# Transposing token rows a second time in float32r, and adding the scaled difference to them

## The chip, the cores and the metric

The kernel runs on one core of one Trainium2 chip. The core has a matrix engine (TensorE, PE in the profile, its weight loads listed apart as PEld), a vector engine (VectorE, DVE), a scalar engine (ScalarE, ACT), a general one (GpSimd, POOL) and a queue that issues transfers (SyncE, SP). Each engine works through its own instructions in order, and semaphores make one wait for another. The metric is the device time of one execution in microseconds.

## What is computed

Eight batches of eight heads of causal attention with a decay from the gates f, over 576 tokens with 64 dimensions a head; then, on the 4608 tokens with their 512 features, a layer norm, two weight matrices with a ReLU between them, and a residual.

```python
scores = np.matmul(q, k.transpose(0, 1, 3, 2)) / np.sqrt(D)
cum = np.cumsum(np.log(np.clip(f, 0.0001, 1.0)), axis=-1)
scores = np.where(causal, -1e9, scores + cum[..., :, None] - cum[..., None, :])
attn = np.exp(scores - scores.max(-1, keepdims=True))
attn = attn / (attn.sum(-1, keepdims=True) + 1e-09)
x = matmul(attn, v)                       # then [tokens, heads * D]
xn = (x - mu) / np.sqrt(var + 1e-06) * g_ln
out = x + np.maximum(xn @ w_ch1, 0.0) @ w_ch2
```

All inputs are float32 but for the two weight matrices, which come as 64-bit floats.

## The kernel before

**Precision.** Most products are made of three float32r products (high times high, high times low, low times high), with each operand split into a rounded high part and the rest. float32r is a second type of four bytes; the kernel rounds an operand into it to get the high part. The first twelve heads use plain float32 or a mixture.

**The attention stage** is a loop over units: 64 heads with four units each, in order. A unit makes the scores of a block of query rows (`qk_mm`, L371 and L372), the mask and the row minimum on VectorE (`softmax_a`, L395), the exponential on ScalarE (L406), the row factor on VectorE (L411, L412), the scaling of the probabilities on GpSimd (L413), their transposes on TensorE two units later (`transpose_unit`, through `tr`, L419), the copies of those on ScalarE (L469) and their low parts on VectorE (L474), and the product with v one unit after that (`av_unit`, L504). Finished heads go to DRAM with features on rows, tokens along the columns (`xd1`, `xd2`).

**The expert stage** (class `Moe`) works through 18 chunks of 256 tokens and is woven into the units: each unit from the 35th on also carries one of a chunk's 16 steps. A step is twelve products into a tile h (`mm1`, L581 to L583), a ReLU on ScalarE (L589), the low part on VectorE (L594), and six products into two accumulators (`mm2`, L603 to L605). A chunk's operand x is loaded from DRAM and split (`chunk_split`, L565 on ScalarE and L566 on VectorE), the last two of its four parts right ahead of the chunk's first step. After the last unit a short loop makes the steps that are left, alone.

**The rows.** The residual and the variance need the tokens with tokens on partitions. After the 9th and the 11th step of a chunk `rows_load` fetches 128 tokens into `xw`, after the 11th and the 13th `chunk_rows` transposes them: four 128x128 transposes into one PSUM bank xp (through `tr`, L419), a copy to xt on ScalarE (L628), and the statistics on VectorE (L633, L634). In all 36 times. After the 13th step `chunk_rstd` queues the fourteen small VectorE operations of the reciprocal root, of which each unit runs up to six; `chunk_out` (L662) scales the accumulators, adds xt and sends the rows out.

**The order** of the work inside a unit is written by hand, as a string of letters. From the 70th unit on it is the last of these; R is the place of `chunk_rows` and of the splits of x, B of the row factor, t of the transposes, A of the product with v, M and N of a step's two groups of products:

```python
    (70, "WwAthQFlMSPNgreamLRB"),
```

**PSUM.** Two banks hold the accumulators. The six others are handed out in turn by `bank`, to scores (s), transposes (tr, xp), products with v (o) and steps (h); a tile waits until the readers of the bank's last tile are done.

```python
    def bank(name):
        return ps.tile([P, 512], F32, tag="b", bufs=6, name=name)
```

`identr` is the identity in float32r, and `ident` the same bytes read as float32. The weights are decoded and split during the first 270 us or so, on ScalarE, VectorE and GpSimd.

Of the kernel before, what the change touches and what calls it, by code (L numbers as in the profile page):

```python
# [8 lines left out]
F32 = mybir.dt.float32  # L9
F32R = mybir.dt.float32r  # L10
# [3 lines left out]
ALU = mybir.AluOpType  # L14

B, H, S, D = 8, 8, 576, 64
DM, DFF = H * D, 4 * H * D
P = 128
KT = DM // P
# [40 lines left out]
def attn_moe(ctx: ExitStack, tc: tile.TileContext, qk, v, f, g, w1, w2, out):  # L60
    nc = tc.nc
# [7 lines left out]
    late = ctx.enter_context(tc.tile_pool(name="late", bufs=1))  # L69
# [3 lines left out]
    def bank(name):  # L73
        return ps.tile([P, 512], F32, tag="b", bufs=6, name=name)

    def m2(name, dt):
        return work.tile([P, 512], dt, tag="m2", bufs=11, name=name)


    identr = const.tile([P, P], F32R, tag="identr", name="identr")  # L80
# [6 lines left out]
    for i in range(WARM):  # L87
# [4 lines left out]
        out=mask[:, S - P :], in_=mask[:, S - P :], pattern=[[-1, P]], base=0,  # L92
# [42 lines left out]
    class WPrep:  # L135
# [132 lines left out]
        late = None  # L268
# [148 lines left out]
    def tr(out_, in_):  # L417
        m = in_.shape[0]
        nc.tensor.transpose(out_, in_, ident[:m, :m])  # L419
# [202 lines left out]
    def chunk_rows(c, i):  # L622

        tp = bank(f"xp{c.n}_{i}")
        for k in range(KT):
            tr(tp[:, P * k : P * k + P], c.xw[:, k, :])
        xt = m2(f"xt{c.n}_{i}", F32)
        nc.scalar.copy(out=xt, in_=tp)  # L628
        if i == 0:
            c.sv = work.tile([P, 2, 2], F32, tag="sv", bufs=2, name=f"sv{c.n}")  # L630
            c.rs = work.tile([P, 4], F32, tag="rs", bufs=2, name=f"rs{c.n}")
        bs = work.tile([P, 6], F32, tag="bs", bufs=2, name=f"bs{c.n}_{i}")
        nc.vector.bn_stats(bs, xt)  # L633
        nc.vector.bn_aggr(c.sv[:, i, :], bs)  # L634
        c.xt.append(xt)
# [30 lines left out]
    class Moe:  # L666
# [62 lines left out]
        def rest(self):  # L729
            c, self.step = self.step, None  # L730
            if c is not None:
                self.prev = (c, c.pend)
                if c.j in (FT - 5, FT - 3):
                    chunk_rows(c, (c.j - (FT - 5)) // 2)
                if c.j in (FT - 7, FT - 5):
                    rows_load(c, (c.j - (FT - 7)) // 2)
                if c.j == FT - 3:
                    chunk_rstd(c)
            self.fetch()
# [160 lines left out]
```

## Time and profile before

| | us |
|---|---|
| median of two runs | 1233.5 (1232.73 to 1234.27) |
| the profiled execution | 1235.2 |
| its span, first to last instruction | 1233.4 |
| TensorE busy | 1209.6 |
| VectorE busy | 763.8 |
| ScalarE busy | 647.0 |
| GpSimd busy | 425.6 |

A profile shows one execution. A group's row gives the source line, engine, operation, output and inputs by the names in the program, the shape, how many there were, then the busy time in microseconds, the mean of one in nanoseconds, the idle time of the engine just before them, and what ended that. A row of the timeline gives start, duration and instruction, merged where several of one kind follow each other ("x4"), with idle time ahead of it in square brackets. TensorE's instructions overlap in the pipeline: the distance from one start to the next says what an instruction costs in a row of them, its own duration does not. L12 is line 12 of the kernel.

The share of busy time in 40 slices of the span shows the stages: weights and attention in the first nine or so, attention with steps up to the 33rd, steps alone behind that.

```profile
PE   7998999899999999999999999999999999999998
DVE  5777647576767667676767676858676765233232
ACT  5887655455556555555555555656555653112111
POOL 3558544234343334344434333434434330000000
PEclk8998999999999999999999999999999999999999
```

### The profile page before, as it was taken

What the parts mean: (1) busy time and instruction counts of PE and PEld (TensorE: products, weight loads), DVE (VectorE), ACT (ScalarE), POOL (GpSimd) and SP (SyncE); (2) the same over time, 40 slices, a digit from 0 to 9 for tenths busy, and PEclk for the clock granted to TensorE, in tenths of its full rate; (3) what the DMA queues carried; (4) which work ended last, traced back from release to release, by engine and by line L of the source; (5) the groups of instructions that cost most, each with busy time, mean ns of one, the idle gap of its engine ahead of it and who ended that gap; (6) DMA issues with size and microseconds to landing.
All of it is one profiled execution on the core that took longest, in us unless ns stands there. A gap on an engine that the chain in (4) does not pass through costs nothing.

```text
span 1233.4 us, 25519 instructions
## 1 busy us (share of the span) xinstructions
PE 1209.6 (98%) x8140; PEld 1079.6 (88%) x8140; DVE 763.8 (62%) x2884; ACT 647.0 (52%) x1920; POOL 425.6 (35%) x533
## 2 busy tenths in 40 slices
PE   7998999899999999999999999999999999999998
PEld 5665889789999999999999999999999999999997
DVE  5777647576767667676767676858676765233232
ACT  5887655455556555555555555656555653112111
POOL 3558544234343334344434333434434330000000
PEclk8998999999999999999999999999999999999999
DMA  6877644444544454455444545545444553443533
GB/s 174 248 231 226 209 146 136 128 162 141 156 144 155 155 172 155 149 164 168 143 143 150 166 155 160 164 126 175 141 145 148 162 155 97 138 132 112 151 110 95
DMA packets 138358, 190.78 MB, mean 155 GB/s; under 512 B 31216, under 2 KB 80624, under 8 KB 138224
## 3 DMA queue, kind: packets, MB, share of 16 engines
q1 hardware_dynamic: 138224, 189.15, 49.7%
q8 instruction: 65, 1.06, 0.4%
q14 instruction: 69, 0.57, 0.2%
HBM read 157.46 MB, written 23.36 MB: 147 GB/s over the span
## 4 chain that ended last, share of the span: by engine, by line
PE 91%; DVE 3%; DMA 2%; ACT 2%; SPq 1%; issue 1%; POOL 0%; DVEq 0%; ACTq 0%; POOLq 0%
PE h L581 11%; PE h L582 11%; PE h L583 11%; PE acc L603 11%; PE acc L604 10%; PE acc L605 10%; PE tr L419 7%; PE o L504 6%; PE s L371 3%; PE s L372 3%; PE o L482 3%; PE s L369 2%; DMA raw<-in_qk_dram 1%; PE xp L419 1%; PE pc L190 1%; DMA wr<-in_w_dram 1%
## 5 line engine op out<-in xcount | busy, mean ns | idle before, releaser
L413 POOL TENSOR_SCALAR p<-p,st 64x64 f32<-64x64 f32 (+4 forms) x320 | 172.2, 541 | 550.2 <-DVE st L412 203.5
L581 PE MATMUL h<-x,w1h 128*128 128x256 f32 x1152 | 330.3, 287 | 5.6 <-DVE st L411 4.1
L582 PE MATMUL h<-x,w1h 128*128 128x256 f32 x1152 | 326.2, 283 | 0.7 <-DVE st L411 0.6
L583 PE MATMUL h<-x,w1l 128*128 128x256 f32 x1152 | 325.4, 282 | 0.0
L589 ACT ACTIVATE hh<-h 128x256 fp32r<-128x256 f32 x288 | 110.5, 384 | 280.2 <-PE h L583 276.2
L594 DVE SCALAR_TENSOR_TENSOR hh<-h,hh 128x256 fp32r<-128x256 f32 x288 | 121.6, 422 | 188.9 <-ACT hh L589 183.5
L603 PE MATMUL acc<-w2h,hh 128*128 128x512 f32 x576 | 228.1, 396 | 0.0
L581 PEld LDWEIGHTS h<-x,w1h 128*128 128x128 f32 x1152 | 218.6, 190 | 10.6 <-DVE st L411 4.3
L604 PE MATMUL acc<-w2s,hh 128*128 128x512 f32 x576 | 226.8, 394 | 0.0
L605 PE MATMUL acc<-w2h,hh 128*128 128x512 f32 x576 | 226.2, 393 | 0.0
L582 PEld LDWEIGHTS h<-x,w1h 128*128 128x128 f32 x1152 | 218.8, 190 | 4.2 <-DVE x L566 1.1
L583 PEld LDWEIGHTS h<-x,w1l 128*128 128x128 f32 x1152 | 218.5, 190 | 0.0
L406 ACT ACTIVATE p<-p,st 64x64 f32<-64x64 f32 (+4 forms) x320 | 178.3, 558 | 56.7 <-DVE st L395 53.7
L469 ACT CAST ph<-tr 64x128 fp32r<-64x128 f32 (+4 forms) x416 | 117.9, 332 | 127.3 <-PE tr L419 98.3
L419 PE MATMUL tr<-identr,p 128*128 128x128 f32 (+1 forms) x896 | 141.8, 275 | 2.6 <-POOL p L413 2.5
L395 DVE CUSTOM_DVE_ANT_0 p<-s,mask 64x64 f32<-64x64 f32 (+4 forms) x320 | 130.4, 420 | 8.8 <-PE tr L419 2.8
L474 DVE TENSOR_TENSOR ph<-tr,ph 64x192 fp32r<-64x192 f32 x208 | 62.6, 301 | 113.1 <-ACT ph L469 110.2
L605 PEld LDWEIGHTS acc<-w2h,hh 128*128 128x128 f32 x576 | 108.4, 188 | 25.6 <-DVE st L411 0.2
L419 PEld LDWEIGHTS tr<-identr,p 128*128 128x128 f32 (+1 forms) x896 | 101.7, 131 | 26.0 <-POOL p L413 5.9
L604 PEld LDWEIGHTS acc<-w2s,hh 128*128 128x128 f32 x576 | 109.3, 190 | 12.4
L603 PEld LDWEIGHTS acc<-w2h,hh 128*128 128x128 f32 x576 | 109.0, 189 | 12.5
L371 PE MATMUL s<-hi 128*64 128x64 f32 x336 | 110.2, 350 | 5.2 <-POOL hi L349 5.2
(82 smaller groups left out, 1790.9 us busy)
## 6 DMA issues: line engine op xcount, KB each, us to landing
w2s<-w2d SPq DMA_DIRECT2D x288, 256.0 KB
raw<-in_qk_dram SPq DMA_DIRECT2D x56, 576.0 KB
wr<-in_w_dram SPq DMA_DIRECT2D x32, 512.0 KB
vr<-in_v_dram SPq DMA_DIRECT2D x64, 160.0 KB
out_dram<-xt SPq DMA_DIRECT2D x36, 256.0 KB
xq<-hi SPq DMA_DIRECT2D x56, 144.0 KB
xa<-xs SPq DMA_DIRECT2D x32, 160.0 KB
w2d<-wl SPq DMA_DIRECT2D x16, 256.0 KB
```

What stands on the lines that cost most here:

```text
L371: mm(sp, h.hi[:, 0, q0 : q0 + m], h.hi[:, 1, a:z], start=True, stop=False)
L395: nc.vector.tensor_tensor_reduce(out=pt[:m, a:z], in0=sp, in1=mask[:m, off + a : off + z], scale=-SCALE, scalar=3.0e38 if i == 0 else st[: ...
L406: nc.scalar.activation(pt[:m, :w], pt[:m, :w], AF.Exp, bias=st[:m, i : i + 1], scale=-1.0, accum_out=st[:m, 2:3])
L413: nc.gpsimd.tensor_scalar(out=pt[:m, :w], in0=pt[:m, :w], scalar1=st[:m, 3:4], scalar2=1.0, op0=ALU.mult, op1=ALU.mult)
L419: nc.tensor.transpose(out_, in_, ident[:m, :m])
L581: mm(ph, w1h[:, k, fs], c.x[k][:, 0, :], start=(k == 0), stop=False)
L582: mm(ph, w1h[:, k, fs], c.x[k][:, 1, :], start=False, stop=False)
L583: mm(ph, w1l[:, k, fs], c.x[k][:, 0, :], start=False, stop=(k == KT - 1))
L594: nc.vector.scalar_tensor_tensor(out=h[:, 1, :], in0=ph, scalar=0.0, in1=h[:, 0, :].bitcast(F32), op0=ALU.max, op1=ALU.subtract)
L603: mm(c.acc[i], h[:, 0, ts_], w2h[:, j, :], start=(j == 0), stop=False)
L604: mm(c.acc[i], h[:, 0, ts_], low, start=False, stop=False)
L605: mm(c.acc[i], h[:, 1, ts_], w2h[:, j, :], start=False, stop=(j == FT - 1))
```

## The change

`chunk_rows` transposes the same rows a second time, into a second bank xq, with data, identity and output declared as float32r. VectorE then subtracts xt, the copy of the first transposes, from it, multiplies the difference by 2^20 and adds it to xt, ahead of the statistics. `dif` is a new SBUF tile of its own.

```diff
         tp = bank(f"xp{c.n}_{i}")
         for k in range(KT):
             tr(tp[:, P * k : P * k + P], c.xw[:, k, :])
+        tq = bank(f"xq{c.n}_{i}")
+        for k in range(KT):
+            nc.tensor.transpose(tq[:, P * k : P * k + P].bitcast(F32R), c.xw[:, k, :].bitcast(F32R), identr)
         xt = m2(f"xt{c.n}_{i}", F32)
         nc.scalar.copy(out=xt, in_=tp)
+        dif = late.tile([P, DM], F32, tag="dif", bufs=1, name=f"dif{c.n}_{i}")
+        nc.vector.tensor_tensor(out=dif, in0=tq, in1=xt, op=ALU.subtract)
+        nc.vector.scalar_tensor_tensor(out=xt, in0=dif, scalar=2.0**20, in1=xt, op0=ALU.mult, op1=ALU.add)
         if i == 0:
```

TensorE's order around the first half of chunk 5 (acc are the accumulators, o the product with v of head 31, tr the transposes of head 32). Before:

```order
L605 MATMUL acc5_1_6641<-w2h_126,hh5_9_7113 128x512
L419 MATMUL xp5_0_7172<-identr_74,xw5_0_7050 128x128 x4
L504 MATMUL o31_4_7198<-ph2_31_7066,vv31_6986 128x256 x4
L504 MATMUL o31_4_7198<-ph2_31_7066,vv31_6986 128x128
L504 MATMUL o31_4_7198<-pl2_31_7067,vv31_6986 64x256 x3
```

Changed:

```order
L605 MATMUL acc5_1_6721<-w2h_126,hh5_9_7193 128x512
L419 MATMUL xp5_0_7252<-identr_74,xw5_0_7130 128x128 x4
L629 MATMUL xq5_0_7257<-identr_74,xw5_0_7130 128x128 x4
L504 MATMUL o31_4_7286<-ph2_31_7146,vv31_7066 128x256 x4
L504 MATMUL o31_4_7286<-ph2_31_7146,vv31_7066 128x128
L504 MATMUL o31_4_7286<-pl2_31_7147,vv31_7066 64x256 x3
```

The four new transposes stand between the old ones and the product with v; nothing else moves.

VectorE's order at the same place (bs and sv are the statistics, st the row factors, ph and pl the transposed probabilities). Before:

```order
L594 SCALAR_TENSOR_TENSOR hh5_10_7168<-h5_10_7144,hh5_10_7168 128x256
L633 BN_STATS bs5_0_7181<-xt5_0_7177 128x6
L634 BN_AGGR sv5_7179<-bs5_0_7181 128x2
L411 TENSOR_SCALAR st32_2_7158<-st32_2_7158 128x1
L412 RECIPROCAL st32_2_7158<-st32_2_7158 128x1
```

Changed:

```order
L594 SCALAR_TENSOR_TENSOR hh5_10_7248<-h5_10_7224,hh5_10_7248 128x256
L633 TENSOR_TENSOR dif5_0_7264<-xq5_0_7257,xt5_0_7262 128x512
L634 SCALAR_TENSOR_TENSOR xt5_0_7262<-dif5_0_7264,xt5_0_7262 128x512
L639 BN_STATS bs5_0_7269<-xt5_0_7262 128x6
L640 BN_AGGR sv5_7267<-bs5_0_7269 128x2
L411 TENSOR_SCALAR st32_2_7238<-st32_2_7238 128x1
L412 RECIPROCAL st32_2_7238<-st32_2_7238 128x1
```

The two new operations stand ahead of the statistics, and so ahead of the row factors of the unit.

## The prediction

> **What bounds the kernel now.** I read the page's head and its chain of waits first, then the busy time by stretch, then who waited on TensorE, and only then single places.
>
> ```profile
> span 1233.4 us, 25519 instructions
> ...
> PE 1209.6 (98%) x8140; PEld 1079.6 (88%) x8140; DVE 763.8 (62%) x2884; ACT 647.0 (52%) x1920; POOL 425.6 (35%) x533
> ...
> PE 91%; DVE 3%; DMA 2%; ACT 2%; SPq 1%; issue 1%; POOL 0%; DVEq 0%; ACTq 0%; POOLq 0%
> ```
>
> The chain that ended last runs on TensorE (PE) for 91% of the span. The next view gives busy time by stretch: length, then PE, weight loads (PEld), VectorE (DVE), ScalarE (ACT), GpSimd (POOL), the granted clock, and DMA.
>
> ```profile
> 280.00:1030.00 750.00, 749.92 (x5297) 690.93 (x5296) 520.42 (x2015) 432.81 (x1310) 289.64 (x366) 1.00 0.49 153
> 1030.00:1233.00 203.00, 199.67 (x1291) 181.47 (x1289) 60.11 (x184) 36.67 (x94) 0.00 (x0) 1.00 0.41 121
> ```
>
> From 280 us on PE has no gap worth the name, in the attention stage (to 1030 us) or behind it. What PE ever waited for lies earlier, and the two longest entries of its waits are small:
>
> ```profile
> PE s L371 <- POOL hi L349: 5.2, 2, 3.6
> PE h L581 <- DVE st L411: 4.1, 1, 4.1
> ```
>
> So a microsecond added to PE's queue is a microsecond on the end, nearly everywhere. The changed step, the rows' transposes, stands in that queue 36 times: 18 chunks of two 128-token halves, four transposes each.
>
> **The change, part 1: four more transposes on PE, 36 times.** First the form that is there already, by line and shape, then the chain around 509 us.
>
> ```profile
> L419 PE MATMUL xp<-identr,xw 128*128 128x128 f32 x144 | 21.6, 272 | 0.0
> 508.83 0.44 PE xp L419 x4
> 509.27 0.95 PE o L504 x9
> ```
>
> One transpose is listed with 272 ns, but they overlap: in the chain four of them take 0.44 us, 0.11 each, and the next group starts right behind. The float32r form is not in the trace. Its pieces are: a float32r weight load of 128 columns, and 128 moving columns in float32r.
>
> ```profile
> 502.06 0.27 PE L372 MATMUL s<-kl,xq 66*128 66x192 f32 x1
> 502.17 0.31 PE L581 MATMUL h<-x,w1h 128*128 128x256 f32 x1
> 502.08 0.19 PEld L581 LDWEIGHTS h<-x,w1h 128*128 128x128 f32 x1
> 502.19 0.19 PEld L582 LDWEIGHTS h<-x,w1h 128*128 128x128 f32 x1
> L504 PE MATMUL o<-pl,vv 128*64 128x128 f32 x104 | 23.1, 222 | 0.0
> 509.64 0.57 PE L504 MATMUL o<-pl,vv 128*64 128x256 f32 x4
> 510.05 0.27 PE L419 MATMUL tr<-identr,p 128*64 128x128 f32 x1
> ```
>
> The first four are float32r products and loads. Loads of 128 columns follow each other at 0.11 us, and a product with only 192 moving columns is also followed after 0.11 (502.06 to 502.17), while 64 columns fewer should have bought something: the load paces it. The last three give the other end. Four float32r products with 64-column loads span 0.57 us; the last is one of 0.222, so it starts at 509.64 + 0.57 - 0.222 = 509.99, and the next instruction starts at 510.05, 0.06 us later. So a float32r transpose costs 0.11 us if its load takes the usual step or if it moves its data as the float32 one does, and 0.06 if neither holds. I take 0.11: both nearest rows, the transpose and the 128-column load, give it, and 0.06 needs a load of half the width.
>
> PE's term: 36 x 4 x 0.11 = 15.8 us; lower end 36 x 4 x 0.06 = 8.6 us. None of it is hidden after 280 us (32 of the 36 halves); of the four earlier ones one sits ahead of the 4.1 us wait above and may vanish, 0.4 us at most.
>
> The Trainium skill ("TensorE: Matmul & The Clock Gate", Part 4: PE-mode transpose) gives about 275 ns for one 128x128 transpose inside a kernel. The 272 ns above agree with it as a duration. Taken as PE's time for each, it would make 144 x 0.275 = 39.6 us, an estimate from that page; the chain's 0.44 us for four speaks against using it so.
>
> **Part 2: two VectorE operations, 36 times.** The subtraction reads one PSUM and one SBUF operand of 128x512; the multiply-add reads two from SBUF.
>
> ```profile
> L474 DVE TENSOR_TENSOR pl<-tr,ph 128x384 fp32r<-128x384 f32 x104 | 58.0, 558 | 2.4
> L474 DVE TENSOR_TENSOR pl<-tr,ph 128x256 fp32r<-128x256 f32 x52 | 22.1, 425 | 1.6
> L662 DVE SCALAR_TENSOR_TENSOR xt<-acc,rs,xt 128x512 f32<-128x512 f32 x36 | 25.5, 745 | 2.0 <-PE acc L605 2.0
> ```
>
> 128 columns more cost 558 - 425 = 133 ns, so the subtraction is 558 + 133 = 691 ns; the multiply-add I price as L662, 745 ns. Together 1.43 us, 51.7 us in all. DVE goes from 764 to 815 us, 65% of the longer span: on average there is room. The place matters more. Around the second half of one chunk (ACT copy, DVE, PE, by time):
>
> ```profile
> 518.01 0.59 ACT L628 COPY xt<-xp 128x512 f32<-128x512 f32 x1 [0.54 <-PE xp L419]
> 518.63 0.69 DVE L633 BATCH_NORM_STATS2 bs<-xt 128x6 f32<-128x512 f32 x1 [1.65 <-ACT xt L628]
> 519.61 0.16 DVE L412 RECIPROCAL st<-st 128x1 f32<-128x1 f32 x1
> 519.96 0.75 POOL L413 TENSOR_SCALAR p<-p,st 128x576 f32<-128x576 f32 x1 [5.08 <-DVE st L412]
> 519.06 0.30 PE L581 MATMUL h<-x,w1h 128*128 128x256 f32 x1
> 521.89 0.60 PE L419 MATMUL tr<-identr,p 128*64 128x128 f32 x4
> 522.00:532.00 10.00, 10.00 (x73) 9.31 (x72) 9.27 (x38) 6.72 (x23) 4.96 (x6) 1.00 0.25 71
> 531.33 0.75 DVE L566 TENSOR_TENSOR x<-xr,x 128x256 fp32r<-128x256 f32 x2
> 531.80 0.39 PE L582 MATMUL h<-x,w1h 128*128 128x256 f32 x1
> DVE ph L474 <- ACT ph L469: 0.8, 1, 0.8
> DVE hh L594 <- ACT hh L589: 0.5, 1, 0.5
> ```
>
> DVE waits 1.65 us for the ACT copy ahead of the statistics, so it arrives there on time whatever the first half cost it. Then it has 2.3 us of work where it had 0.9, and 1.43 us more stand ahead of two hand-overs to PE.
>
> The first is the tightest. The row statistics (L412) release GpSimd's normalisation of the probabilities, which ends at 519.96 + 0.75 = 520.71; PE transposes them at 521.89, 1.18 us later. There is no idle time on this way, so GpSimd ends 1.43 us later, and PE, itself 0.44 later by then, finds 1.18 - 1.43 + 0.44 = 0.19 us left. It holds, barely, at the second half of each chunk.
>
> The second: behind 522 us DVE is nearly full, 9.27 of 10 us. At the end of that stretch the next chunk's operand x is split (L566, two of them; the first ends about 531.33 + 0.375 = 531.7) and PE reads it at 531.80, 0.1 us later. The lateness of 1.43 - 0.44 = 0.99 us shrinks by DVE's idle time on the way; the last two rows are DVE's waits between 510 and 538 us apart from those for the copy, 0.8 + 0.5 = 1.3 us, so x should come in time.
>
> Both margins are a tenth or two wide. I allow 0.5 us in all for chunks where they fail. Upper end: half of 0.99 us in each of the 13 chunks of the attention stage, 6.4 us; lower end 0, since nothing here can make PE's work shorter. Behind 1030 us DVE is busy for 60 of 203 us and covers the 1.43 us.
>
> **Part 3: one more PSUM buffer per half.** The six shared banks go round faster: between xp and the next use of the same bank there is one tile fewer. The bank of xp is wanted next by the h tile at 519.06, and the copy that frees it ends at 518.60; PE comes 0.44 us later now, so that gap grows. The bank of xq is free when the subtraction ends, 518.63 + 0.69 = 519.32, and the next tile in it is written at 521.89 (plus 0.44). Cost 0. If the copy were later by a microsecond, PE would stall that long at 519.06.
>
> Part 4: nothing is added on ACT, POOL or the DMA queue, and nothing is moved past another instruction. ACT's copy waits for xp alone, not for xq.
>
> **The sum.** 15.8 + 0.5 + 0 = 16.3 us. The profiled execution took 1235.2 us (span 1233.4 and 1.8 around it), which gives 1251.5; it stands 1.7 us above the median of 1233.5, so against the median the forecast is 1249.8 us, 1.3% slower. A measurement of this kernel can tell about 2% (24.7 us) from no change, so this counts as within it.
>
> **Rivals.**
> - *The fast transpose.* Float32r needs one pass and a short load: 0.06 us each, 8.6 us, 1242.1. For it: the 64-column rows above. Against it: every 128-column float32r load here steps at 0.11.
> - *DVE takes over (slower).* If DVE's idle time on the way is not really idle, because ACT and DVE wait on each other in turn, each of the 26 halves of the attention stage (13 chunks) shows its 0.99 us on PE: 25.7 us more, 1275. For it: 9.27 of 10 us busy, and margins of 0.19 and 0.1 us. Against it: 1.3 us of waits on the way, and a DVE that is 70% busy over the stage (520 of 750 us). It decides from 0.34 us a half, when 1249.3 passes 1258.2.
> - *Transposes that do not overlap.* Each float32r transpose holds PE for its 272 ns: 144 x 0.272 = 39.2 us, 1272.7. This is what the Trainium skill's 275 ns (same page and part as above) would come to. Against it: float32 transposes overlap, and so do float32r products.
> - *It is hidden.* PE's ends are modelled, so its 749.92 of 750 us could contain slack: 1233.5. For it: the loads are busy for 691 of 750 us only. Against it: the chain steps from one matmul to the next without a gap.
>
> **How the numbers follow.** 0.11 us a transpose with stalls below 6.4 us: 0.68, and its own range is 1249 to 1256. Fast transpose: 0.16. DVE takes over: 0.09. No overlap: 0.04. Hidden: 0.03. The range 1241 to 1256 holds the first two (0.84) and leaves out the rest (0.16); its low end is the fast transpose's 1242 and 1 us for the run-to-run spread, its high end 1249.3 + 6.4. Slower by over 2%: DVE and no overlap, 0.13. Faster by over 2%: 0.01, for what I have not seen. Within 2%: 0.86.
>
> **What would show it.** Four xq transposes on the chain with 0.44 us (0.24 for the fast one, 1.1 without overlap). The subtraction at about 0.69 and the multiply-add at about 0.75 us. PE busy in the attention stage as before, with no waits on GpSimd's p or DVE's x beyond a few tenths; a row "PE tr <- POOL p" or "PE h <- DVE x" of many microseconds would be the DVE rival. The statistics' wait for the copy should now stand ahead of the subtraction with the same 1.6 us. I am wrong if PE's busy time grows by 16 us and the span does not, or the other way round.

## The result and the profile after

| | before | changed |
|---|---|---|
| median | 1233.5 us (1232.73 to 1234.27, 2 runs) | 1254.2 us (1253.46 to 1254.95, 2 runs) |
| the profiled execution, its span | 1235.2, 1233.4 us | 1254.95, 1253.2 us |
| TensorE, VectorE busy | 1209.6, 763.8 us | 1225.8, 812.6 us |

The ratio is 1.0169, interval 1.0146 to 1.0191: 20.7 us slower, and by the measure of 2% no change that counts. The forecast was 1249.8 us with 1241 to 1256.

The head of the page of the changed kernel and the shares of its chain of waits:

```profile
span 1253.2 us, 25915 instructions
...
PE 1225.8 (98%) x8284; PEld 1091.2 (87%) x8284; DVE 812.6 (65%) x2956; ACT 644.8 (51%) x1920; POOL 424.9 (34%) x533
...
PE 80%; DVE 7%; DMA 6%; ACT 3%; issue 2%; SPq 2%; POOL 1%; DVEq 0%; POOLq 0%; ACTq 0%
```

TensorE's busy time grew by 16.2 us and the span by 19.8. The chain now runs on TensorE for 80% instead of 91%, and the largest part of the rest that any compute engine took up is VectorE's, 7% instead of 3%; transfers went from 2% to 6%. These shares tell where the chain ran, not what a step cost. TensorE's busy time isn't all work either: the same 8140 instructions as before are listed with 1212.7 and 1219.9 us in two of the runs below. The two added kinds of work, in the view of groups by line and shape:

```profile
L629 PE MATMUL xq<-identr,xw 128*128 128x128 f32 x144 | 19.3, 258 | 0.0
L633 DVE TENSOR_TENSOR dif<-xq,xt 128x512 f32<-128x512 f32 x36 | 24.9, 692 | 46.9 <-ACT xt L631 45.1 <-PE s L372 1.0 <-PE o L504 0.9
L634 DVE SCALAR_TENSOR_TENSOR xt<-dif,xt 128x512 f32<-128x512 f32 x36 | 26.1, 726 | 1.2
L639 DVE BATCH_NORM_STATS2 bs<-xt 128x6 f32<-128x512 f32 x36 | 25.0, 695 | 1.2
```

The wait for ScalarE's copy stands ahead of the subtraction now, 45.1 us in 36 halves; the multiply-add and the statistics follow it with almost no idle time. The subtraction lasts what was forecast (0.691 us). The multiply-add was priced at 0.745 us; 35 of the 36 take 0.69, and one takes 1.92, hence the mean.

**Where the time went, by stage.** Two marks divide each trace: the first product (L581) of chunk 2 and that of chunk 14. Between them lie 12 chunks, 24 halves, all but the last beside attention; behind the second lie 8 halves alone. The rows of the tile view at the two marks, each cut to a window that begins with the mark, give count, shortest/median/longest in ns, and first and last start in us. Before:

```profile
L581 PE MATMUL h<-x,w1h x2: 283/283/283, 270.7 to 271.1; 128*128 128x256 f32 x2
L581 PE MATMUL h<-x,w1h x2: 278/280/282, 1045.0 to 1045.3; 128*128 128x256 f32 x2
```

Changed:

```profile
L581 PE MATMUL h<-x,w1h x2: 282/284/285, 274.4 to 274.7; 128*128 128x256 f32 x2
L581 PE MATMUL h<-x,w1h x2: 278/280/282, 1061.8 to 1062.2; 128*128 128x256 f32 x2
```

| us | start to chunk 2 | chunk 2 to 14 | chunk 14 to the end |
|---|---|---|---|
| before | 270.7 | 774.2 | 188.4 |
| changed | 274.4 (+3.6) | 787.4 (+13.2) | 191.4 (+2.9) |

The first stage holds four of the 36 halves and varies between executions: it took 266.4 to 276.4 us over all the profiles below, and 274.4 and 271.7 in two of the changed kernel, so its 3.6 us say little. In the last stage 2.9 us over 8 halves is 0.36 us each. In the middle it is 13.2 over 24, 0.55 each. Something costs there that doesn't cost at the end.

What the weight loads (PEld) waited for between 290 and 1090 us, in the view of waits (total us, times, longest). Before:

```profile
PEld o L504 <- DVE ph L474: 0.4, 1, 0.4
PEld h L582 <- DVE x L566: 0.3, 1, 0.3
```

Changed:

```profile
PEld tr L419 <- POOL p L413: 3.7, 13, 0.7
PEld o L504 <- DVE ph L474: 1.9, 4, 0.8
PEld h L582 <- DVE x L566: 2.2, 5, 0.8
```

0.7 us became 7.8. These are waits of the loads; TensorE's products are listed with 1.8 us of waits there, and neither figure is the cost, which the stage gives. All three are hand-overs behind the added VectorE work: the probabilities p (by way of the row factor and GpSimd), their transposed high part ph, and the next chunk's operand x. How it goes at one place, the second half of chunk 5, in the timeline of the changed kernel:

```profile
526.62 0.69 DVE L633 TENSOR_TENSOR dif<-xq,xt 128x512 f32<-128x512 f32 x1 [1.54 <-ACT xt L631]
527.34 0.69 DVE L634 SCALAR_TENSOR_TENSOR xt<-dif,xt 128x512 f32<-128x512 f32 x1
529.41 0.75 POOL L413 TENSOR_SCALAR p<-p,st 128x576 f32<-128x576 f32 x1 [5.42 <-DVE st L412]
530.26 0.60 PE L419 MATMUL tr<-identr,p 128*64 128x128 f32 x4
534.23 0.80 PE L504 MATMUL o<-ph,vv 128*128 128x256 f32 x5 [0.16 <-DVE ph L474]
540.85 0.41 DVE L566 TENSOR_TENSOR x<-xr,x 128x256 fp32r<-128x256 f32 x1
541.32 0.38 PE L582 MATMUL h<-x,w1h 128*128 128x256 f32 x1 [0.61 <-DVE x L566]
```

GpSimd ends p at 529.41 + 0.75 = 530.16 and TensorE transposes it at 530.26: that hand-over holds by 0.10 us. Then TensorE waits 0.16 us for ph, and 0.61 for x seven microseconds after that.

### The profile page after: what moved, and what is told of

Its sections match the earlier page's. It is cut to its first block, busy times and chain, and to the rows that moved or that the text cites. A ratio compares the mean times of both kernels' runs of the same rounds, so it can differ in the third digit from the quotient of the medians.

```text
span 1253.2 us, 25915 instructions
## 1 busy us (share of the span) xinstructions
PE 1225.8 (98%) x8284; PEld 1091.2 (87%) x8284; DVE 812.6 (65%) x2956; ACT 644.8 (51%) x1920; POOL 424.9 (34%) x533
## 4 chain that ended last, share of the span: by engine, by line
PE 80%; DVE 7%; DMA 6%; ACT 3%; issue 2%; SPq 2%; POOL 1%; DVEq 0%; POOLq 0%; ACTq 0%
PE h L581 9%; PE h L582 9%; PE h L583 9%; PE acc L603 9%; PE acc L604 9%; PE acc L605 9%; PE tr L419 6%; PE o L504 5%; DMA raw<-in_qk_dram 3%; PE o L482 3%; PE s L371 3%; PE s L372 3%; PE s L369 2%; DMA xr<-xa 2%; DVE p L395 1%
## 5 line engine op out<-in xcount | busy, mean ns | idle before, releaser
L581 PE MATMUL h<-x,w1h 128*128 128x256 f32 x1152 | 330.4, 287 | 1.0 <-ACT xs L535 0.7
L581 PEld LDWEIGHTS h<-x,w1h 128*128 128x128 f32 x1152 | 218.8, 190 | 5.9 <-ACT xs L535 1.0
L395 DVE CUSTOM_DVE_ANT_0 p<-s,mask 64x64 f32<-64x64 f32 (+4 forms) x320 | 130.4, 420 | 6.2 <-PE s L372 1.9
```

The costliest lines, as they stand in the source:

```text
L395: nc.vector.tensor_tensor_reduce(out=pt[:m, a:z], in0=sp, in1=mask[:m, off + a : off + z], scale=-SCALE, scalar=3.0e38 if i == 0 else st[: ...
L581: mm(ph, w1h[:, k, fs], c.x[k][:, 0, :], start=(k == 0), stop=False)
```

## The experiments

Two theories stood against each other: that what lies above TensorE's own work is VectorE's lateness at these hand-overs, or that it is the transposes themselves (or their PSUM bank). A third, that it is chance from the uneven start, is answered by the stages: behind the start a half costs 0.55 us, and in the last stage 0.36. Each run was timed beside runs of the kernel before on the same chip, whose medians were 1234.3 to 1234.9 us. "Stage" below is chunk 2 to 14 and "tail" is chunk 14 to the end, each against the profile of before.

**The change once more.** No edit.

> The changed kernel again, beside the kernel before on the same chip: +20 us (+18 to +22) by every theory. In the profile of the change the second transposes shift the work behind them by about 0.36 us a half (36 x 0.36 = 13), so some 6 to 7 us stand besides. Theory 1: these are hand-overs from VectorE to TensorE that come late. Theory 2: they are TensorE's own, by the seventh tile that goes round six banks. Theory 3: they are chance, from the uneven first 250 us.

1255.1 us, ratio 1.0154 (1.0132 to 1.0176). Stage +16.4, tail +2.9. The tail repeats to a tenth; the stage differs by 3.2 us between two executions of one program, so a difference of that size between profiles means nothing there.

**The transposes alone.**

```diff
-        dif = late.tile([P, DM], F32, tag="dif", bufs=1, name=f"dif{c.n}_{i}")
-        nc.vector.tensor_tensor(out=dif, in0=tq, in1=xt, op=ALU.subtract)
-        nc.vector.scalar_tensor_tensor(out=xt, in0=dif, scalar=2.0**20, in1=xt, op0=ALU.mult, op1=ALU.add)
```

> Keeps the second transposes and their bank, leaves out the subtraction and the multiply-add (so nothing is added to the rows). Theory 1: +13 us over before (12 to 15). Theory 2: +19 to +21, as much as the whole change. Theory 3: +13, and the whole change not surely above it.

1247.93 us, ratio 1.0093 (1.0074 to 1.0112), 13.0 us over the kernel before. Stage +8.4, which is 0.35 us a half, tail +2.9, which is 0.36: the same price in both. No wait of TensorE or its loads is listed between 290 and 1090 us. On the page TensorE's busy time has grown by the same 13.0 us, from 1209.6:

```profile
span 1246.0 us, 25818 instructions
...
PE 1222.6 (98%) x8284; PEld 1092.0 (88%) x8284; DVE 763.8 (61%) x2884; ACT 647.0 (52%) x1920; POOL 423.6 (34%) x533
```

So four float32r transposes cost 0.36 us, 0.09 each, and the second bank nothing. (Nothing reads that bank here. In the run with the subtraction alone, below, VectorE reads it, and no wait for it is listed there either.)

**The VectorE operations alone**, on the rows themselves.

```diff
-        tq = bank(f"xq{c.n}_{i}")
-        for k in range(KT):
-            nc.tensor.transpose(tq[:, P * k : P * k + P].bitcast(F32R), c.xw[:, k, :].bitcast(F32R), identr)
-        nc.vector.tensor_tensor(out=dif, in0=tq, in1=xt, op=ALU.subtract)
+        nc.vector.tensor_tensor(out=dif, in0=xt, in1=xt, op=ALU.subtract)
```

> Leaves out the second transposes and their bank, keeps the two VectorE operations, with the rows themselves in place of the second transposes (so the difference is zero). Theory 1: TensorE is not late itself here, so the lateness at each hand-over is the full 1.4 us and not 1.07: +6 to +15 us over before, more than the rest of the whole change. Theories 2 and 3: 0 to +1.

1247.23 us, ratio 1.0102 (1.0082 to 1.0122), 12.3 us with nothing added on TensorE. Stage +12.7, tail 0.0. The loads' waits between 290 and 1090 us:

```profile
PEld tr L419 <- POOL p L413: 11.8, 16, 1.1
PEld o L504 <- DVE ph L474: 2.8, 4, 1.1
PEld h L582 <- DVE x L566: 2.7, 7, 0.8
```

Two operations on an engine that is busy for 65% of the span cost one per cent, all of it where attention runs beside. The two parts alone add up to 25.3 us and together give 20.2 (the repeated change beside the same runs). That fits the first theory: the transposes make TensorE later, and the lateness of VectorE against it smaller.

**The second transposes in float32.**

```diff
-            nc.tensor.transpose(tq[:, P * k : P * k + P].bitcast(F32R), c.xw[:, k, :].bitcast(F32R), identr)
+            tr(tq[:, P * k : P * k + P], c.xw[:, k, :])
```

> The second transposes in float32 instead of float32r, everything else as in the change. By the spacing in the profiles (0.109 us each against 0.09): 36 x (0.44 - 0.36) = +2.9 us over the change by every theory; theory 1 takes up to 1 us off that, since TensorE comes later to the hand-overs. 0 if the type makes no difference to TensorE.

1255.66 us, ratio 1.0165 (1.0141 to 1.0188); 0.6 over the repeated change by the medians where some 2 to 3 were expected; the intervals of the two overlap. The tail tells the two forms apart: +3.7 us, 0.46 a half, against 0.36. Stage +16.3: four dearer transposes a half should add 24 x 0.10 = 2.4 us, but VectorE's lateness shrinks with them, and the spread of the stage hides the rest. The loads' waits speak for it: in the two profiles of the change they waited 3.7 and 4.0 us for p, 13 times each, and here 0.2 us, once, with TensorE 0.1 us a half later.

**The subtraction alone** beside the transposes.

```diff
-        nc.vector.scalar_tensor_tensor(out=xt, in0=dif, scalar=2.0**20, in1=xt, op0=ALU.mult, op1=ALU.add)
```

> The change without the multiply-add (the difference is made and added to nothing): 0.69 us of VectorE a half instead of about 1.4. Theory 1: lateness relative to TensorE falls from about 1.07 to 0.33 us, so nearly all of the rest goes: +12 to +14 us over before, like the transposes alone. Rival (any added VectorE operation, or the use of the second bank by VectorE, costs the rest): half to all of the 7 us stays, +16 to +19.

1247.14 us, ratio 1.0108 (1.0087 to 1.0128): the median is that of the transposes alone. The profiled execution is a long one, 1251.5 us, and has stage +11.1, 2.7 over the transposes alone, with few waits of the loads: 0.6 us for ph, 0.5 for x and 0.7 for other things. Half the VectorE work is nearly free.

**Twice the VectorE work**: the subtraction three times.

```diff
         nc.vector.tensor_tensor(out=dif, in0=tq, in1=xt, op=ALU.subtract)
+        nc.vector.tensor_tensor(out=dif, in0=tq, in1=xt, op=ALU.subtract)
+        nc.vector.tensor_tensor(out=dif, in0=tq, in1=xt, op=ALU.subtract)
```

> The change with the subtraction made three times (same result): 2.8 us of VectorE a half. Theory 1: lateness relative to TensorE rises from 1.07 to 2.45 us, past every margin; at 26 halves of the attention stage the added 1.38 us shows in part or in full: 10 to 36 us over the change, +30 to +55 over before. Rival (the rest does not come from VectorE's time): within 3 us of the change.

1282.87 us, ratio 1.0392 (1.0372 to 1.0411). Stage +39.5, tail +3.4. TensorE's and its loads' waits between 290 and 1090 us:

```profile
PEld tr L419 <- POOL p L413: 34.6, 22, 2.3
PE tr L419 <- POOL p L413: 25.1, 22, 1.8
```

The busy time of one stretch (length, PE, PEld, DVE, ACT, POOL, clock, DMA):

```profile
500.00:560.00 60.00, 57.55 (x410) 52.54 (x409) 45.49 (x166) 33.77 (x102) 21.02 (x28) 1.00 0.50 152
```

The same stretch with the transposes alone:

```profile
500.00:560.00 60.00, 60.00 (x430) 55.35 (x429) 41.99 (x165) 35.25 (x107) 22.09 (x30) 1.00 0.52 165
```

TensorE idles 2.45 of 60 us while VectorE is 76% busy (45.49 of 60). It isn't VectorE's throughput that runs out, it is its lateness at one hand-over. The doses side by side, with a half's added VectorE time, less the 0.36 us that TensorE itself is later (the three subtractions and the multiply-add take 0.69 us each):

| run | lateness added a half | cost a half in the stage, over the transposes' own |
|---|---|---|
| subtraction alone | 0.69 - 0.36 = 0.33 us | 2.7 / 24 = 0.11 us (by the medians 0) |
| the change, two profiles | 1.42 - 0.36 = 1.06 | 4.8 to 8.0 / 24 = 0.20 to 0.33 |
| VectorE operations alone | 1.42 | 12.7 / 24 = 0.53 |
| three subtractions | 2.77 - 0.36 = 2.41 | 31.1 / 24 = 1.30 |

From the third row to the fourth 0.99 us more of lateness cost 0.77 us; the first 0.33 cost 0.11 or nothing. By these rows a half absorbs some tenths, up to about 0.7 us (1.42 less 0.53 / 0.78), and passes on some three quarters of the rest.

**The row factor ahead of the rows' work**, on the kernel with the VectorE operations alone. If the wait for p is all, the row factor placed first should take it away.

```diff
-    (70, "WwAthQFlMSPNgreamLRB"),
+    (70, "WwAthQFlMSPNgreamLBR"),
```

> The VectorE operations without the second transposes, as in the run of the vector part alone (+12.5 us there), but from unit 70 on the row factor stands ahead of the rows' work in a unit (R and B swapped), so that GpSimd's probabilities no longer wait for it. In the trace of the vector part alone, some 8 of its 12.7 us after 280 us came at transposes of probabilities, 2.5 at the first step of a chunk, 2 at products with v. Theory 1: +3 to +7 over before. If the lateness only moves to the next hand-over: +10 to +13.

A miss: 1254.98 us, ratio 1.0156 (1.0135 to 1.0177), 20.2 us slower than before and not 12.3. Stage +18.1. The wait for p is gone, and others have come (290 to 1090 us; `tr_4b` is a transpose tile, and L395 the row minimum, whose work reads its PSUM bank's last tile):

```profile
PE tr_4b L419 <- DVE st L395: 5.5, 11, 0.5
PEld tr_4b L419 <- PE tr L419: 7.8, 11, 0.7
PEld h L582 <- DVE x L566: 5.4, 11, 0.8
PEld o L504 <- DVE ph L474: 3.2, 5, 0.9
```

They are not only the old lateness at other places. With the row factor first, GpSimd scales p while VectorE works on the rows, and here both last longer. At the second half of chunk 5, where p takes 0.75 us and the multiply-add 0.69 in the run with the VectorE operations alone:

```profile
530.71 0.69 DVE L630 TENSOR_TENSOR dif<-xt 128x512 f32<-128x512 f32 x1
531.43 1.12 DVE L631 SCALAR_TENSOR_TENSOR xt<-dif,xt 128x512 f32<-128x512 f32 x1
530.78 1.23 POOL L413 TENSOR_SCALAR p<-p,st 128x576 f32<-128x576 f32 x1 [2.55 <-PE s L372]
```

On average the multiply-add lasts 915 ns and the subtraction 829, against 695 and 721 in that run: 0.33 us more a half. The scaling of 128x576 lasts 852 against 752. In the tail, where GpSimd is idle, both VectorE operations stay at 0.69 us. How much of the 7.9 us over that run is lateness that moved, and how much comes from operations that grew, the run doesn't tell.

**The same order in the kernel before**, to see what the move costs by itself.

> The kernel before with R and B swapped from unit 70 on, as in the run with the row factor first, and nothing else: the control for that run (+19 us). If the swap by itself does nothing (-1 to +1), the excess of that run over the vector part alone (7 us) is lateness that met later hand-overs. If the swap costs 4 us or more by itself, the run told nothing of where lateness goes.

1234.22 us in 12 runs beside 1234.26, ratio 1.0003 (0.9988 to 1.0017), stage +0.1. Alone the move is free. But the two operations that grew are not in this kernel (the split of x is, with 488 ns on average instead of 436), so it doesn't rule their growth out as the cause.

**The statistics later.** In the changed kernel the two statistics operations go to the list of small operations that the next unit runs, so that 0.87 us less (0.695 and 0.18) stands ahead of the row factor.

```diff
-        nc.vector.bn_stats(bs, xt)
-        nc.vector.bn_aggr(c.sv[:, i, :], bs)
+        later.append(lambda: nc.vector.bn_stats(bs, xt))
+        later.append(lambda: nc.vector.bn_aggr(c.sv[:, i, :], bs))
```

> The change with its two statistics operations (0.87 us) taken out of the rows' place and queued with the small operations that each next unit runs; VectorE's total is the same. Theory 1: VectorE is late by 1.4 - 0.9 - 0.36, about 0.2 us, at GpSimd's probabilities, so those waits (3.7 us of the change's weight loads) go; the work still stands ahead of the split of x, so the waits there (about 4 us with the products with v) stay: +14 to +17 over before. Rival (VectorE's total counts, wherever it stands, as in the run with the factor first): +19 or more.

A miss by the median: 1253.02 us, ratio 1.016 (1.0135 to 1.0184), stage +16.0, tail +3.0. It is 18.8 us over before, between the two forecasts, and the interval reaches into both; 20.2 for the repeated change is hardly more. Between 290 and 1060 us the wait for p is off the list again, and x is at its head:

```profile
PEld h L582 <- DVE x L566: 4.9, 8, 1.2
PEld o L504 <- DVE ph L474: 1.9, 4, 0.8
```

VectorE's busy time is that of the change (812.7 and 812.6 us), so here the added work did not grow: the lateness changed its place.

**The same, with the low half of x on GpSimd**, so that neither p nor x waits for VectorE.

```diff
-        nc.vector.tensor_tensor(out=x[:, 1, :], in0=xr, in1=x[:, 0, :].bitcast(F32), op=ALU.subtract)
+        nc.gpsimd.tensor_tensor(out=x[:, 1, :], in0=xr, in1=x[:, 0, :].bitcast(F32), op=ALU.subtract)
```

> As the run with the statistics later, and the low half of x is made on GpSimd instead of VectorE. Theory 1: waits for x fall too, TensorE keeps only its own 13 us: +12 to +15 over before. If GpSimd, slower at this, hands x over later than VectorE did: +16 or more, with the wait now on GpSimd.

1257.05 us, ratio 1.0189 (1.0163 to 1.0215), stage +15.7: no gain, as the expectation's second case had it. The split by groups, first here and then in the run above, each with its own idle time, and then the waits between 290 and 1060 us here:

```profile
L566 POOL TENSOR_TENSOR x<-xr,x 128x256 fp32r<-128x256 f32 x72 | 52.6, 741 | 221.1 <-ACT x L565 172.2 <-DMA w2s<-w2d 43.1 <-DMA xr<-xa 2.1
```

```profile
L566 DVE TENSOR_TENSOR x<-xr,x 128x256 fp32r<-128x256 f32 x72 | 30.4, 444 | 20.3 <-ACT x L565 20.1
```

```profile
PEld h L582 <- POOL x L566: 4.8, 14, 0.6
```

The split takes 741 ns on GpSimd and 444 on VectorE, so x is late again, from another engine. Nor did VectorE gain what it gave away: 30.4 us of splits left it, and its busy time fell from 812.7 to 807.9 us only, as small operations grew (54 of the reciprocal root's from 191 to 349 ns on average). The run doesn't tell whether VectorE's lateness would have shown at a third place if x had been on time.

**The later statistics in the kernel before.**

> The kernel before with its statistics queued in the same way, the control for the run with the statistics later: TensorE has no wait in the attention stage to lose, so 0 (-1 to +1) by every theory.

1233.13 us in 12 runs, ratio 0.9997 (0.9985 to 1.0009), stage +1.1. Free by the medians, though its loads wait 1.6 us for x where those of before wait 0.3. So neither the other order nor the later statistics costs time of its own by the medians. Of the two runs that used them, only that with the later statistics shows the lateness changing its place, since nothing else grew there. (The split of x on GpSimd was not tried in the kernel before.)

**The rows in float32r only**: the kernel before, with its one set of the rows' transposes in the second type, and nothing added.

```diff
-            tr(tp[:, P * k : P * k + P], c.xw[:, k, :])
+            nc.tensor.transpose(tp[:, P * k : P * k + P].bitcast(F32R), c.xw[:, k, :].bitcast(F32R), identr)
```

> The kernel before, with its own row transposes in float32r instead of float32 and no second set. By the spacing of the two forms: 36 x (0.44 - 0.36) = -2.9 us against before (-4 to -1). Rival: 0, if the type only matters behind another transpose.

1232.08 us in 12 runs beside 1234.81 in 17, ratio 0.998 (0.9969 to 0.9992): 2.7 us faster than the kernel before, the fastest here, and the interval ends below 1. Tail -0.6, which is 0.075 us a half, and 36 of those would be 2.7. The stage has only -0.8 where 24 of them would be 1.8, a difference within its spread. In the tail's timeline, four transposes to the next product; in this run

```profile
1208.94 0.45 PE L626 MATMUL xp<-identr,xw 128*128 128x128 f32 x4
1209.23 0.35 PE L581 MATMUL h<-x,w1h 128*128 128x256 f32 x1
```

and before

```profile
1213.22 0.60 PE L419 MATMUL xp<-identr,xw 128*128 128x128 f32 x4
1213.58 0.36 PE L581 MATMUL h<-x,w1h 128*128 128x256 f32 x1
```

0.29 us against 0.36, from start to start: 0.07 saved, the same size as by the tail. (Only the difference counts here: four more transposes cost 0.36 and 0.46 us in the tail.)

## Why the prediction held, and where it didn't

The time lies in the range, and in the likeliest case's own range of 1249 to 1256, but 4.4 us above the forecast. Two terms of the sum were off, in opposite directions, and that it lies within the range is in part luck: the stalls found below, 4.8 to 8.0 us, on top of the forecast's own 15.8 for the transposes would have made 1254.1 to 1257.3, the upper part of it outside.

- *Four transposes at 0.11 us.* Mis-sized: 0.36 us for four, 0.09 each; where 0.44 were to show, the changed kernel's timeline at the first half of chunk 5 has 0.38 from start to start:

```profile
516.65 0.54 PE L629 MATMUL xq<-identr,xw 128*128 128x128 f32 x4
517.03 0.76 PE L504 MATMUL o<-ph,vv 128*128 128x256 f32 x5
```

  That makes 36 x 0.36 = 13.0 us where the sum had 15.8; the transposes alone took 13.0 by the medians as well. "The load paces it" put the float32r transpose at the step of a 128-column load, but these loads aren't the ones quoted. In the changed kernel's tile view (ns) they are shorter than the products' 190:

```profile
L629 PEld LDWEIGHTS xq<-identr,xw x144: 139/140/143, 173.8 to 1239.3; 128*128 128x128 f32 x144
```

  The float32 transposes' loads take 140 ns as well, and those transposes cost 0.11, so the load alone doesn't set the price; what does stays open. The true value lies between the two ends that the prediction kept, 0.06 and 0.11; neither nearest row was the operation. That none of it is hidden was right (0.35 and 0.36 a half), so the rivals of a hidden change and of the fast transpose (8.6 us) fell. The sign that PE's busy time grows by 16 us came out as 16.2, but the transposes alone added 13.0 of it.

- *Stalls of 0.5 us in all.* This step failed. The sentence was that the lateness of 0.99 us "shrinks by DVE's idle time on the way", 1.3 us, "so x should come in time". At the very chunk from which it was read, x came 0.61 us late. The 1.3 us were misread. They are the waits between 510 and 538 us, and the longer one lies ahead of the added work, which starts at 518.63. Before, with its two waits, and then the one on the way in the changed kernel:

```profile
514.72 0.28 DVE L474 TENSOR_TENSOR ph<-tr,ph 64x128 fp32r<-64x128 f32 x1 [0.82 <-ACT ph L469]
521.96 0.42 DVE L594 SCALAR_TENSOR_TENSOR hh<-h,hh 128x256 fp32r<-128x256 f32 x1 [0.49 <-ACT hh L589]
```

```profile
531.49 0.42 DVE L594 SCALAR_TENSOR_TENSOR hh<-h,hh 128x256 fp32r<-128x256 f32 x1 [0.58 <-ACT hh L589]
```

  So 0.49 us stood on the way and not 1.3; with the margin of 0.1 it left x 0.4 us late even if all of it had shrunk. It did not shrink. From the first operation on the rows to the split of x VectorE took 12.70 us before (518.63 to 531.33) and 14.23 in the changed kernel (526.62 to 540.85), 1.53 more; the added operations alone make 1.45 of it (526.62 to 528.07). ScalarE made hh later, too: its instruction ahead of it, L338, waited 1.99 us for a transfer where it had waited 0.81. Why that transfer came later stays open. Over the stage the lateness cost 13.2 - 8.4 = 4.8 us in the profile above and 16.4 - 8.4 = 8.0 in the repeated one, against an upper end of 6.4. The margin of the first hand-over was read well, 0.19 us forecast and 0.10 found at that chunk; but it is a margin of one chunk, and transposes elsewhere in the stage waited for p 13 times.

- *Tail covers the VectorE work*: right, 0.0 us with those operations alone.

- *The bank costs nothing*: right; with the transposes alone TensorE waits for nothing in the stage, and where the subtraction reads the bank no wait for it is listed.

- *DVE takes over.* Its mechanism was real, and its size wrong: 0.20 to 0.33 us a half and not 0.99, below the 0.34 from which it was said to decide. Doubling the work carried it over: 1.30 us a half and 3.9% slower.

- *No overlap.* Wrong: the transposes lasted 258 ns each and cost 0.09. The Trainium skill's 275 ns ("TensorE: Matmul & The Clock Gate", Part 4: PE-mode transpose) is near the durations in this trace (258 and 272 ns) and is no price on TensorE's queue.

The sum with the measured terms: 13.0 + 4.8 to 8.0 = 17.8 to 21.0 us, and 20.7 were measured (20.2 in the repetition). What stays open is which hand-over would be last if all of p, ph and x were on time. Each rearrangement freed p and met x and ph, two of the three made other operations longer on the way, and none freed them all.

## What to carry to other kernels

An average says little of the room on an engine that feeds the bound one: VectorE was busy for 62% of the span, and 1.4 us of work in front of a hand-over still cost TensorE 0.2 to 0.5 us each time, while 0.7 us cost almost nothing. Count the margin at every hand-over behind the added work, over all its occurrences rather than at one. An idle stretch of the late engine helps only if it lies between the added work and the hand-over, and only if what ends it doesn't come later as well. Moving the work past one hand-over can deliver the lateness to the next, and it changes what the work runs beside: compare the durations of the moved operations before reading the waits. And a part alone, in both halves (the engine's own work without the helper's, the helper's without the engine's), told the two terms apart that the sum of the change had mixed.

## What the hardware showed that was not expected

A float32r transpose of 128x128 costs TensorE 0.09 us in a row of them (0.36 / 4, the tail and the stage alike) and a float32 one 0.11 (0.46 / 4 in the tail): the same transposes of the same rows, a fifth cheaper in the other type. The weight loads of the transposes take 140 ns where those of the products with as many columns take 190. One VectorE subtraction of 128x256 takes 444 ns on average where GpSimd takes 741. And with the row factor first, a VectorE operation with both inputs in SBUF and GpSimd's scaling of p both lasted longer when they met: 1.12 us instead of 0.69, and 1.23 instead of 0.75.
